# Transposes into an unread bank in TensorE's planned pauses, in the first part of the program

## The chip, the cores and the metric

The kernel runs on one core of a Trainium2 chip. The metric is the device time of one execution in microseconds, as the median of several runs. Five engines work side by side, each through a list of its own in order: TensorE (PE, with its weight loads shown as PEld), VectorE (DVE), ScalarE (ACT), GpSimd (POOL) and SyncE (SP), which here only issues DMAs.

## The reference

Attention with a causal mask and a decay bias, for 8 batches of 8 heads, 576 positions and a head width of 64, and behind it a feed-forward layer with an ELU between two products.

```python
cum = np.cumsum(np.maximum(s, 0.0), axis=-1)
bias = -(cum[:, :, :, None] - cum[:, :, None, :])
scores = np.where(causal, -1e9, q @ k.T / 8 + np.minimum(bias, 0.0))
attn = softmax(scores)                 # 576 x 576 for each head
x = (attn @ v)                         # heads side by side: 4608 x 512
h = x @ w_in                           # 512 x 2048
g = np.where(h > 0, h, np.exp(np.minimum(h, 0)) - 1)
out = g @ w_out                        # 2048 x 512
```

## The kernel before

The program has two kinds of work. Attention goes unit by unit. A unit is one batch and one pair of heads, or one head of it. The first three batches have their first 320 rows done as twelve "low" units in plain f32 (`prepare_low`, `scoring_low`, `weighing_low`), four to a batch; the remaining rows and batches follow as other units. The feed-forward layer goes in 12 chunks of 384 tokens (`moe_chunk`), each over 16 blocks of 128 hidden columns (`hidden`, line 1165, and `project`, line 1203). Products of the chunks stand between those of the later attention units and fill TensorE there. The first low units have no chunk work beside them yet, since no chunk's input is ready.

A low unit goes through these steps:

- SP loads keys (`kl`), queries (`ql`) and values (`vs`), and the row of decay sums for the keys (`kl<-aux` for the second unit, `kl<-aux_dram` after it). POOL fills the constant rows (lines 412 and 605). For the first unit DVE works out the sums itself (`kl_first`, lines 430 to 434).
- TensorE makes five score tiles `sc` of widths 128, 192, 192, 320 and 320 (line 869). DVE adds the mask and takes the minimum (line 872), ACT takes the exponential and the row sum (line 877), DVE inverts the sums (lines 882 and 883), and POOL, DVE or ACT scale the weights (lines 890, 892 and 894).
- TensorE turns the weights (`trl`, lines 680 and 694: transposes by `ident`), ACT or DVE copy them to `tl` (lines 381 and 382), and TensorE multiplies them by the values (`avl`, line 675). The weighing of a unit stands between the scores of the next one.

Beside this, the weights `w_in` and `w_out` are loaded in 32 pieces and split into two parts each, with several instructions on DVE, ACT and POOL for a piece (lines 363 to 374 and 531 to 537).

The order of all of it is planned when the program is built. `op` records an operation with the engines that could do it and their costs in nanoseconds; `Plan.issue` keeps a clock for each engine, takes the operation that could start earliest (a lower `prio` first among equals) and writes it behind the last one of its engine. Operations are held in order by that list, and a wait on a semaphore is added for each dependency on another engine. A buffer of one tag becomes free when the last user of its holder has been planned. Score tiles may borrow the banks of PSUM of the feed-forward part while those are idle:

```python
def score_bank(name):
    return plan.buf(ps, [P, 512], F32, name, tag="a", bufs=N_A,
                    others=[("h", N_H), ("o0", 1), ("o1", 1), ("o2", 1)])
```

So there are seven banks for scores and turned weights in the first part, two each of `a` and `h` and one each of `o0`, `o1` and `o2`, and an eighth for `avl`.

The constant `ident` is written by POOL at the start of the program, before anything of the plan.

Of the kernel before, what the change touches and what calls it, by code (L numbers as in the profile page):

```python
# [9 lines left out]
F32 = mybir.dt.float32  # L10
# [7 lines left out]
P = 128  # L18
# [26 lines left out]

N_FREE = 0


class Buf:

# [17 lines left out]


class Op:  # L70
    __slots__ = ("ways", "after", "before", "behind", "bufs", "new", "prio", "ready", "left")


class Plan:
# [33 lines left out]
    def op(self, prio, ways, reads=(), writes=(), late=()):  # L108

        o = Op()  # L110
        o.ways, o.prio = ways, (prio, len(self.ops))
        o.after, o.before, o.behind, o.bufs, o.new = set(late), [], [], set(), []
        firsts = set()
        for accesses, write in ((reads, False), (writes, True)):
            for a in accesses:
                b, part = a if isinstance(a, tuple) else (a, None)
                if not b.parts and b not in o.bufs:

                    n = self.tags.get(b.key, 0)
                    self.tags[b.key] = n + 1  # L120
                    o.new.append((b, n))
                    b.first = o
                firsts.add(b.first)
                if b not in o.bufs:
                    o.bufs.add(b)
                    b.users += 1
                for key, (writers, readers) in b.parts.items():
                    if part is None or key is None or key == part:
                        o.after.update(writers)
                        if write:  # L130
                            o.after.update(readers)
                writers, readers = b.parts.setdefault(part, ([], []))
                if write:
                    if part is None:
                        b.parts = {None: ([o], [])}
                    else:
                        b.parts[part] = ([o], [])
                else:
                    readers.append(o)
        o.after.discard(o)  # L140
        firsts -= o.after | {o}
        for d in o.after:
            d.before.append(o)
        for d in firsts:
            d.behind.append(o)
        o.left, o.ready = len(o.after) + len(firsts), {}
        self.ops.append(o)
        return o
# [8 lines left out]
    def issue(self):  # L157
        engines = sorted({self.ENGINE.get(w[0], w[0]) for o in self.ops for w in o.ways})
        port = 0.0
        free = dict.fromkeys(engines, 0.0)  # L160
# [12 lines left out]
        pending = [o for o in self.ops if not o.left]  # L173
        block = self.nc.cur_bb.bb
        last = {}
        n_done = 0
        while pending:
            best = None
            held = slots.get(self.signal, ())
            busy = free["PE"] > DYN_T or held and held[-1].users and not held[-1].others  # L180
            for o in pending:
                t = 0.0
                for b, k in o.new:
                    at = None
                    if taken[b.home] == k:
                        b.key, b.bufs = b.home, b.home_bufs
                        at = slot_free(b.key, b.bufs)
                    if b.others and not busy:
                        for key, bufs, *most in b.others:
                            if most and taken[key] > most[0]:  # L190
                                continue
                            other = slot_free(key, bufs)
                            if other is not None and (at is None or other < at):
                                at, b.key, b.bufs = other, key, bufs
                    if at is None:
                        break
                    t = max(t, at)
                else:
                    _, n, start = min(
                        (at + w[1] * self.BIAS.get(w[0], 1.0), i, at)  # L200
                        for i, w, at in (
                            (i, w, max(t, free[self.ENGINE.get(w[0], w[0])],
                                       self.ready(o, self.ENGINE.get(w[0], w[0])),
                                       port - self.PORT_LEAD if w[0] in self.PORT else 0.0))
                            for i, w in enumerate(o.ways)
                        )
                    )
                    rank = (start, o.prio)
                    if best is None or rank < best[0]:
                        best = (rank, o, n)  # L210
            assert best is not None, "no operation can be issued"
            (start, _), o, n = best
            engine, cost, trace = o.ways[n][:3]
            lag = 0.0
            end = start + cost
            if engine in self.PORT:
                port = end
            engine = self.ENGINE.get(engine, engine)
            if len(o.ways[n]) > 3:

                pipe = max(pipe, end) + o.ways[n][4] / RATE
                lag = pipe + o.ways[n][3] - end
            self.log.append((engine, start, end, o.prio))
            free[engine] = end
            for b, k in o.new:
                gone = skipped.setdefault(b.home, set())
                gone.add(k)
                while taken[b.home] in gone:
                    gone.remove(taken[b.home])
                    taken[b.home] += 1  # L230
                slots.setdefault(b.key, []).append(b)
            for b in o.bufs:
                b.until = max(b.until, end + lag)
                b.users -= 1
            pending.remove(o)
            for d in o.before:
                d.ready[engine] = max(d.ready.get(engine, 0.0), end + lag)
            for d in o.behind:
                d.ready[None] = max(d.ready.get(None, 0.0), start)
            for d in (*o.before, *o.behind):  # L240
                d.left -= 1
                if not d.left:
                    pending.append(d)
            at = len(block.instructions)
            trace()
            for i in block.instructions[at:]:
                if i.engine in last:
                    self.tc.add_manual_dep(
                        i, last[i.engine],
                        mybir.DependencyInfo(  # L250
                            mybir.DependencyClass.NoSync, mybir.DependencyReason.DATA
                        ),
                        reason="planned order",
                    )
                last[i.engine] = i.name
# [47 lines left out]
def kernel(  # L303
# [28 lines left out]
    DM, DF = w_in.shape  # L332
# [13 lines left out]
    plan = Plan(tc)  # L346
    op = plan.op
# [796 lines left out]
    def moe_chunk(ch, rows, xc, after):  # L1144
# [101 lines left out]
                t += n  # L1246
        return following

    decay_sums()
    zeros()  # L1250
    mask_tiles()
# [94 lines left out]
```

## Time and profile before

| what | value |
|---|---|
| median of 3 runs | 1131.26 us (1130.28, 1131.26, 1135.73) |
| profiled execution | 1133.43 us, of it the span 1131.7 us |
| mean granted TensorE clock of the profiled execution | 0.993 |
| TensorE matmuls: busy, instructions | 1096.9 us, 5992 |
| DVE, ACT, POOL busy | 843.3, 628.1, 451.1 us |
| DMA queue 1: moved, share of 16 engines | 155.27 MB, 59.6% |

The profile is of one execution. Its times count from the start of the span. A row of the timeline shows the start, the time from the first start to the last end of a run of like instructions (with their count behind an x), the engine, the line, and what was written from what; in brackets the idle time before it and what ended it. The runs of a row overlap their neighbours, since matmuls are pipelined. A row of the windows shows how long each engine was busy in a stretch, and the clock that TensorE was granted there as a share of the full one.

### The profile page before, as it was taken

The page shows a single profiled execution, that of the slowest core. Times are in us where ns is not written, and L with a number is a line of the kernel's source. Part 1 is how long each engine was busy: PE and PEld are TensorE (multiplying, and loading weights), DVE is VectorE, ACT ScalarE, POOL GpSimd, SP SyncE. Part 2 cuts the span into 40 slices and gives each one's busy share as a digit, 9 for nine tenths or more (in the row PEclk, how much of TensorE's full clock was granted, in tenths as well). Part 3 has the DMA queues.
Part 4 walks back from the last instruction along what each step waited for, and adds up shares of the span by engine and source line. Part 5 has one row for each costly group of instructions (what it writes and reads, how often), then busy time and mean ns, then how long its engine had stood idle before and what let it go on. Part 6 is the DMA issues. An engine that isn't in the chain of part 4 may idle for free.

```text
span 1131.7 us, 19748 instructions
## 1 busy us (share of the span) xinstructions
PE 1096.9 (97%) x5992; PEld 951.6 (84%) x5992; DVE 843.3 (75%) x2133; ACT 628.1 (55%) x1525; POOL 451.1 (40%) x657
## 2 busy tenths in 40 slices
PE   6888999999999999999999999999999999999998
PEld 5677877888788888788888888888888888999997
DVE  6888999778887877687977787878888888432322
ACT  4786766456555655555555555655655556433433
POOL 6664475336444433344434434525544433100000
PEclk8899999999999999999999999999999999999999
DMA  6887688756756855765555666567787686210000
GB/s 173 225 213 201 172 189 193 157 113 152 161 125 128 186 130 121 180 127 133 149 133 118 175 140 136 122 143 172 160 200 155 138 189 151 56 56 1 28 1 28
DMA packets 341689, 156.52 MB, mean 138 GB/s; under 512 B 266424, under 2 KB 320464, under 8 KB 341584
## 3 DMA queue, kind: packets, MB, share of 16 engines
q1 hardware_dynamic: 341584, 155.27, 59.6%
q8 instruction: 48, 0.79, 0.3%
q14 instruction: 57, 0.47, 0.1%
HBM read 79.66 MB, written 19.32 MB: 87 GB/s over the span
## 4 chain that ended last, share of the span: by engine, by line
PE 63%; DVE 6%; DMA 2%; issue 1%; ACT 1%; POOL 1%; SPq 0%; POOLq 0%; DVEq 0%; ACTq 0%
PE o L1203 26%; PE h L1165 25%; PE av L1000 7%; PE sc L869 5%; DVE p L930 2%; DMA stq<-in_qT_dram 1%; DMA T<-p 1%; DVE p L872 1%; DVE h L1187 1%; DVE xl L374 1%; DVE qs L374 0%; DVE x_None L1084 0%; DVE gl L1190 0%; DVE vs L374 0%; DVE g L1182 0%
## 5 line engine op out<-in xcount | busy, mean ns | idle before, releaser
L1165 PE MATMUL h<-xh,wi 128*128 128x384 f32 x1536 | 445.5, 340 | 1.4 <-DVE gl L1190 1.3
L1203 PE MATMUL o<-wo,gh 128*128 128x512 f32 x1152 | 362.5, 396 | 0.1
L1165 PEld LDWEIGHTS h<-xh,wi 128*128 128x128 f32 x1536 | 283.0, 188 | 9.9 <-DVE gl L1190 3.0
L1165 PE MATMUL h<-xl,wi 128*128 128x384 f32 x768 | 258.8, 337 | 0.0
L1203 PEld LDWEIGHTS o<-wo,gh 128*128 128x128 f32 x1152 | 207.3, 188 | 27.4 <-DVE mn L872 0.5
L1203 PE MATMUL o<-wo,gl 128*128 128x512 f32 x576 | 227.8, 395 | 1.0 <-DVE gl L1190 0.8
L1187 DVE SCALAR_TENSOR_TENSOR h<-h,g 128x384 f32<-128x384 f32 x192 | 107.9, 562 | 122.2 <-ACT g L1178 120.6
L1173 ACT ACTIVATE g<-h 128x384 f32<-128x384 f32 x192 | 94.1, 490 | 177.5 <-PE h L1165 167.4
L877 ACT ACTIVATE p<-p,mn 128x192 f32<-128x192 f32 (+1 forms) x232 | 144.9, 625 | 75.1 <-DVE mn L872 72.0
L930 DVE SCALAR_TENSOR_TENSOR p<-p,sm,p 128x512 f16<-128x512 f32 (+3 forms) x239 | 170.7, 742 | 7.6 <-POOL p L922 4.5
L1165 PEld LDWEIGHTS h<-xl,wi 128*128 128x128 f32 x768 | 144.6, 188 | 6.7
L922 POOL TENSOR_SCALAR p<-p,sm 128x512 f16<-128x512 f32 (+3 forms) x125 | 86.9, 702 | 134.3 <-DVE sm L883 53.1
L381 ACT CAST gh<-h 128x384 fp32r<-128x384 f32 x175 | 83.5, 477 | 87.8 <-DVE h L1187 86.6
L1190 DVE TENSOR_TENSOR gl<-h,gh 128x384 fp32r<-128x384 f32 x192 | 106.0, 552 | 32.9 <-ACT gh L381 31.7
L1203 PEld LDWEIGHTS o<-wo,gl 128*128 128x128 f32 x576 | 108.2, 188 | 25.8 <-DVE gl L1190 2.3
L872 DVE CUSTOM_DVE_ANT_0 p<-sc,maskw 128x192 f32<-128x192 f32 (+1 forms) x232 | 109.8, 483 | 25.8 <-PE sc L869 21.4
L1000 PE MATMUL av<-T,vs 128*128 128x256 f16 (+5 forms) x896 | 119.2, 285 | 2.9 <-DMA T<-p 2.1
L1000 PEld LDWEIGHTS <-vs 128*128 128x128 bf16 x896 | 79.7, 98 | 49.8 <-issue 14.3
L375 POOL TENSOR_TENSOR vs<-vs 128x320 f32<-128x320 f32 x72 | 61.0, 848 | 124.6 <-DMA vs<-in_vb_dram 72.1
L869 PE MATMUL sc<-kh,qs 128*128 128x192 f32 (+2 forms) x272 | 87.5, 326 | 2.9 <-DVE mn L872 2.5
L869 PE MATMUL sc<-k,q 128*128 128x192 f32 (+2 forms) x272 | 83.9, 312 | 2.2 <-DMA q<-qs 1.3
L1178 ACT ACTIVATE g<-g 128x384 f32<-128x384 f32 x138 | 72.5, 525 | 4.2
(145 smaller groups left out, 1365.3 us busy)
## 6 DMA issues: line engine op xcount, KB each, us to landing
stk<-in_kT_dram SPq DMA_DIRECT2D x64, 288.0 KB
vs<-in_vb_dram SPq DMA_DIRECT2D x64, 160.0 KB
stq<-in_qT_dram SPq DMA_DIRECT2D x40, 256.0 KB
w_i<-in_w_in_dram SPq DMA_DIRECT2D x16, 512.0 KB
w_o<-in_w_out_dram SPq DMA_DIRECT2D x16, 512.0 KB
out_dram<-ost SPq DMA_DIRECT2D x32, 256.0 KB
x_dram<-x_None SPq DMA_DIRECT2D x20, 288.0 KB
q<-qs SPq DMA_DIRECT2D x40, 128.0 KB
```

Of the source, the lines that this page charges most:

```text
L381: ("ACT", act_c(n), lambda: act.copy(dst(), src())),
L869: pe_.matmul(view(sc.v[:, :cw]), l, r, start=n == 0, stop=n == len(pairs) - 1)
L872: op(prio, [("DVE", 84 + dve_p(cw), lambda i=i, sc=sc: dve.tensor_tensor_reduce(pt.v[:, i * cw : (i + 1) * cw], sc.v[:, :cw], mv(i * cw, c ...
L877: op(prio, [("ACT", 480 + w / 1.2, lambda: act.activation(pt.v[:, :w], pt.v[:, :w], AF.Exp, bias=mn.v[:, n - 1 : n], scale=-1.0, accum_out ...
L922: ("Pool", 160 + 1.04 * n, lambda part=part: pool.tensor_scalar(part(t16, 0), own(part), sm.v[:, r], 1.0, ALU.mult, ALU.mult)),
L930: ("DVE-SB", dve_2(n), lambda part=part: dve.scalar_tensor_tensor(part(t16, 1), own(part), sm.v[:, r], part(t16, 0), ALU.mult, ALU.subtract)),
L1000: op(prio, [("PE", cost, lambda m=m, operands=operands, rows=rows: pe_.matmul(av.v[:rows, dst], *operands(), start=first and m == 0, stop= ...
L1165: pe_.matmul(hp.v[:, :TC], w_in_f[f].v[:, part, c * P : (c + 1) * P], xx.v[:, c, :TC], start=(c == 0 and m == 0), stop=(c == NCB - 1 and m ...
L1173: op(side, [("ACT", act_c(TC), lambda: act.activation(g.v[:, :TC], hp.v[:, :TC], AF.Exp))], [hp], [g])
L1187: op(side, [("DVE", dve_p(TC), lambda: dve.scalar_tensor_tensor(hp.v[:, :TC], hp.v[:, :TC], 0.0, g.v[:, :TC], ALU.max, join[0]))], [g], [hp])
L1190: op(side, [("DVE", dve_p(TC), lambda: dve.tensor_tensor(gl.v[:, :TC], hp.v[:, :TC], gh.v[:, :TC].bitcast(F32), ALU.subtract))], [hp, gh], ...
L1203: pe_.matmul(acc[i].v, g.v[:, tb], w_out_f[f].v[:, part], start=(f == 0 and m == 0), stop=(f == NF - 1 and m == 2),)
```

## The change

A function `fillers` gives the plan one transpose of `ident` into a tile `scratch` in PSUM, and 300 more of the same that read and write nothing else. They have the lowest urgency, a cost of 160 ns each in the plan, and are ranked 350 ns behind the time at which they could start: one is taken only where no other operation could start within 350 ns of it. Once TensorE's planned clock is past 60 us, those that are left are dropped. Nobody reads `scratch`. Its tag is `o2`, and it has that bank until the leftovers are dropped.

```diff
+FILL_T, GAP = 60e3, 350.0
+
+N_FILL = 300
+
...
-        o.ways, o.prio = ways, (prio, len(self.ops))
+        o.ways, o.prio, o.filler = ways, (prio, len(self.ops)), False
...
         while pending:
+            if free["PE"] > FILL_T:
+                for o in [o for o in pending if o.filler]:
+                    pending.remove(o)
+                    for b in o.bufs:
+                        b.users -= 1
+                if not pending:
+                    break
             best = None
...
-                    rank = (start, o.prio)
+                    rank = (start + GAP if o.filler else start, o.prio)
                     if best is None or rank < best[0]:
                         best = (rank, o, n)
             assert best is not None, "no operation can be issued"
             (start, _), o, n = best
+            if o.filler:
+                start -= GAP
...
+    def fillers():
+
+        scratch = plan.buf(ps, [P, DM], F32, "scratch", tag="o2")
+        op(-20, [("PE", 111.0, lambda: pe_.transpose(scratch.v[:, :P], ident, ident))], [], [scratch])
+        for n in range(N_FILL):
+            o = op(1e6 + n, [("PE", 160.0, lambda: pe_.transpose(scratch.v[:, :P], ident, ident))], [(scratch, None)], [])
+            o.filler = True
+
+    fillers()
     decay_sums()
```

In the built program 77 transposes stand, all on TensorE: 32, 23, 4, 5, 4 and 9 of them at six places. The other rows of TensorE and all rows of DVE, ACT, POOL and SP stand in the order of before. The lines of the changed kernel below are 13 higher than those of before for the same work (882 for 869, 707 for 694, 688 for 675).

TensorE's order at the start of the program, before, with the semaphores that a row waits for in brackets (`sc_0_...` are scores of the first unit, `sc_1_...` of the second, `trl_0` turned weights of the first; the last number of a name only counts tiles):

```order
L869 MATMUL sc_0_0_0_121<-kl_first,ql_0_85 128x128 [waits DMAHW2_49,DMAHW3_49,DVE_49,Pool_49]
L869 MATMUL sc_0_1_0_128<-kl_first,ql_0_85 128x192
L869 MATMUL sc_0_2_0_133<-kl_first,ql_0_85 128x192
L869 MATMUL sc_0_3_0_144<-kl_first,ql_0_85 128x320
L869 MATMUL sc_0_4_0_150<-kl_first,ql_0_85 128x320
L869 MATMUL sc_1_0_0_181<-kl_1_89,ql_1_99 128x128 [waits DMAHW5_49,DMAHW6_49,DMAHW2_49,Pool_49]
L869 MATMUL sc_1_1_0_188<-kl_1_89,ql_1_99 128x192
L869 MATMUL sc_1_2_0_194<-kl_1_89,ql_1_99 128x192 [waits DVE_49]
```

The same place of TensorE's order in the changed kernel:

```order
L1265 MATMUL scratch<-ident 128x128 [waits Pool_49]
L1267 MATMUL scratch<-ident 128x128 x31
L882 MATMUL sc_0_0_0_154<-kl_first,ql_0_93 128x128 [waits DMAHW2_49,DMAHW3_49,DVE_49,Pool_49]
L882 MATMUL sc_0_1_0_161<-kl_first,ql_0_93 128x192
L882 MATMUL sc_0_2_0_166<-kl_first,ql_0_93 128x192
L882 MATMUL sc_0_3_0_177<-kl_first,ql_0_93 128x320
L882 MATMUL sc_0_4_0_183<-kl_first,ql_0_93 128x320
L1267 MATMUL scratch<-ident 128x128 x23
L882 MATMUL sc_1_0_0_237<-kl_1_102,ql_1_115 128x128 [waits DMAHW5_49,DMAHW6_49,DMAHW2_49,Pool_49]
L882 MATMUL sc_1_1_0_244<-kl_1_102,ql_1_115 128x192 [waits DVE_49]
L882 MATMUL sc_1_2_0_250<-kl_1_102,ql_1_115 128x192 [waits DVE_49]
```

32 transposes stand ahead of the first score and wait for POOL alone, 23 stand behind the first unit's scores, and the second score of the second unit now waits for DVE, as its third did before.

TensorE's order at the end of the second unit's weighing, before (`trl_1_2` is the last piece of its turned weights, `avl_1` its products with the values, `sc_3` a score of the fourth unit):

```order
L675 MATMUL avl_1_314<-tl_1_303,vs_92 128x192
L694 MATMUL trl_1_2_354<-ident,p_112 128x128 [waits PE_49]
L694 MATMUL trl_1_2_354<-ident,pl_0_1_135 128x128
L675 MATMUL avl_1_314<-tl_1_303,vs_92 128x64 [waits DVE_49]
L675 MATMUL avl_1_314<-tl_1_303,vs_92 128x64
L869 MATMUL sc_3_0_0_375<-kl_3_246,ql_3_253 128x128 [waits DMAHW7_49,DMAHW6_49,DMAHW0_49]
```

The same place in the changed kernel:

```order
L688 MATMUL avl_1_370<-tl_1_359,vs_106 128x192
L707 MATMUL trl_1_2_410<-ident,p_141 128x128 [waits PE_49]
L707 MATMUL trl_1_2_410<-ident,pl_0_1_168 128x128
L1267 MATMUL scratch<-ident 128x128 x4
L688 MATMUL avl_1_370<-tl_1_359,vs_106 128x64 [waits DVE_49]
L688 MATMUL avl_1_370<-tl_1_359,vs_106 128x64
```

Four transposes stand ahead of the row that waits for DVE's copy of the turned weights.

TensorE's order at the last place, the weighing of the sixth unit, before:

```order
L694 MATMUL trl_1_1_700<-ident,pl_1_1_538 128x128
L694 MATMUL trl_1_1_700<-ident,pl_1_1_546 128x128
L694 MATMUL trl_1_2_717<-ident,p_112 128x128
L694 MATMUL trl_1_2_717<-ident,pl_1_1_546 128x128
L675 MATMUL avl_1_737<-tl_1_688,vs_92 128x128
```

The same place in the changed kernel:

```order
L707 MATMUL trl_1_1_765<-ident,pl_1_1_603 128x128
L707 MATMUL trl_1_1_765<-ident,pl_1_1_611 128x128
L1267 MATMUL scratch<-ident 128x128 x4
L707 MATMUL trl_1_2_786<-ident,p_141 128x128
L707 MATMUL trl_1_2_786<-ident,pl_1_1_611 128x128
L1267 MATMUL scratch<-ident 128x128 x9
L688 MATMUL avl_1_815<-tl_1_753,vs_106 128x128
```

Four transposes stand ahead of the last turned weights and nine behind them. The remaining five stand in the weighing of the fourth unit, between `trl_3` and `trl_3_0`.

More of the change, by code (lines that the diff above doesn't have):

```diff
@@ L70 @@
 class Op:
-    __slots__ = ("ways", "after", "before", "behind", "bufs", "new", "prio", "ready", "left")
+    __slots__ = ("ways", "after", "before", "behind", "bufs", "new", "prio", "ready", "left", "filler")
 class Plan:
```

## The prediction, made before the changed kernel ran

> **What bounds the kernel now.** I read the page first: span, busy engines, the TensorE clock by slice, the chain that ended last.
>
> ```profile
> span 1131.7 us, 19748 instructions
> PE 1096.9 (97%) x5992; PEld 951.6 (84%) x5992; DVE 843.3 (75%) x2133; ACT 628.1 (55%) x1525; POOL 451.1 (40%) x657
> ...
> PEclk8899999999999999999999999999999999999999
> ...
> PE 63%; DVE 6%; DMA 2%; issue 1%; ACT 1%; POOL 1%; SPq 0%; POOLq 0%; DVEq 0%; ACTq 0%
> ```
>
> TensorE bounds the whole, but the clock row is below 9 only in the first two slices (57 us). So I cut that part into windows, with edges moved until each held one clock. Columns: stretch, length, busy time (instructions) of PE, PEld, DVE, ACT, POOL, granted clock, DMA share, GB/s.
>
> ```profile
> 6.65:10.07 3.42, 3.42 (x10) 2.67 (x10) 2.89 (x8) 1.04 (x4) 3.23 (x10) 1.00 0.82 143
> 10.07:13.48 3.41, 0.35 (x2) 0.00 (x0) 3.31 (x13) 1.84 (x7) 1.80 (x4) 1.00 0.35 97
> 13.48:20.31 6.83, 6.12 (x21) 5.26 (x22) 1.78 (x10) 2.67 (x9) 1.12 (x3) 0.50 0.91 257
> 27.13:30.55 3.42, 1.83 (x13) 1.45 (x11) 3.39 (x10) 2.31 (x5) 2.24 (x5) 1.00 0.97 251
> 30.55:37.37 6.82, 6.13 (x22) 5.31 (x22) 3.55 (x13) 3.86 (x14) 3.68 (x6) 0.50 0.91 255
> 37.37:92.00 54.63, 48.95 (x287) 39.41 (x286) 49.19 (x163) 45.70 (x148) 34.55 (x74) 1.00 0.80 206
> ...
> 85.16:88.57 3.41, 2.19 (x15) 1.81 (x14) 3.34 (x8) 2.15 (x9) 2.73 (x8) 1.00 0.35 82
> ...
> 92.00:1131.70 1039.70, 1023.34 (x5606) 891.66 (x5604) 770.63 (x1900) 563.23 (x1321) 393.06 (x524) 1.00 0.59 133
> ```
>
> There are two spells at half clock, 13.48 to 20.31 and 30.55 to 37.37: both 6.83 us long, with starts 17.07 us apart, 2.5 times that length. So the clock is judged on a fixed raster of 3.41 us. The raster window ahead of each spell has little TensorE work: 0.35 us (10%) and 1.83 us (54%). A window with 2.19 us (64%) kept the clock. The limit lies between 54 and 64% busy, that is 1.2 to 1.6 us idle in 3.41 us. From 37 to 92 us the clock holds, and DVE is at 49.19 of 54.63 us (90%), as is PE. After 92 us PE is busy 98%: what the first part gains mostly stays gained.
>
> There is also a first cold burst that the clock column doesn't show.
>
> ```profile
> 6.47 3.95 PE L869 MATMUL sc<-kl_first,ql 128*128 128x128 f32 x10 [6.47 <-DVE kl_first L434]
> 8.31 2.11 PE L869 MATMUL sc<-kl_first,ql 128*128 128x320 f32 x4
> 14.19 2.04 PE L869 MATMUL sc<-kl,ql 128*128 128x128 f32 x6 [3.77 <-POOL p L890]
> ...
> 75.44 0.70 PE L869 MATMUL sc<-kl,ql 128*128 128x320 f32 x2
> ...
> 17.30 0.63 PE L694 MATMUL trl<-ident,p 128*128 128x128 f32 x2
> 17.73 0.63 PE L694 MATMUL trl<-ident,pl 128*128 128x128 f32 x2
> ...
> 61.85 0.38 PE L694 MATMUL trl<-ident,p 128*128 128x128 f32 x2
> 62.07 0.38 PE L694 MATMUL trl<-ident,pl 128*128 128x128 f32 x2
> ```
>
> Four instructions of width 320 take 2.11 us (0.53 each) at 8.31, two take 0.70 us at 75.44 (0.27 each, after about 0.16 of tail): the first five scores run at half pace though the column says 1.00. The transposes give a filler's price by their starts: two in 0.43 us cold (0.21 each), two in 0.22 us warm (0.11 each).
>
> **The change, part by part.** It adds 77 transposes at six places of PE's order and moves no other row on any engine. If TensorE's pace were all, warmth would be worth 1.9 us in the first burst (half of 3.95) and 3.1 us in each spell (half of 6.12 and 6.13), 8.1 us in all. What holds that up:
>
> ```profile
> 1.71 0.29 POOL masks.py:199 TENSOR_SCALAR_AFFINE_SELECT ident<-ident 128x128 f32<-128x128 f32 x1
> 7.40 0.29 DVE L872 CUSTOM_DVE_ANT_0 pl<-sc,masks 128x128 f32<-128x128 f32 x1 [0.53 <-PE sc L869]
> 9.75 0.88 POOL L469 MEMSET k<- 64x576 f32 x1
> 10.50 0.62 SPq L351 DMA_DIRECT2D kl<-in_kT_dram  x1
> 10.58 0.62 POOL L605 MEMSET ql<- 64x640 f32 x1
> 11.13 0.07 DVE L872 DVE_READ_ACCUMULATOR2_ANT mn<- 128x1 f32 x1
> 11.24 0.53 SPq L351 DMA_DIRECT2D ql<-in_qT_dram  x1
> 11.87 0.66 SPq L351 DMA_DIRECT2D kl<-aux  x1
> 12.80 0.15 DVE L882 TENSOR_SCALAR sml<-sml 128x5 f32<-128x5 f32 x1
> 13.92 0.53 POOL L890 TENSOR_SCALAR pl<-pl,sml 128x320 f32<-128x320 f32 x1
> ```
>
> *32 ahead of the first score.* They wait for ident alone, which POOL ends at 2.00. All cold they take 32 x 0.213 = 6.8 us, to 8.9; if a raster edge after 3.41 busy us warms them earliest (5.5 us), 16 cold and 16 warm end at 7.2. So they overrun the first score's start at 6.47 by 0.7 to 2.4 us; the burst, now warm, takes 1.9 to 2.0 and ends at 9.2 to 10.9 against 10.42. DVE's first reduction at 7.40 comes 0.4 to 2.1 us later, and its gapless chain up to the sums at 12.80 with it. This is covered: the last of these weights is ready at 14.45 (POOL at 13.92), and PE takes them at 17.30, 2.85 us later. If the spell goes, half of that cover goes too. Nor is there a gain: the second unit's first score at 14.19 needs the load at 11.87, which stands on SP behind a load that awaits POOL's fill of ql (10.58), and POOL is busy to 10.63 in any case. I take 0, between -0.5 and +0.8.
>
> *23 after the first burst.* Warm they take 23 x 0.107 = 2.5 us of a 3.77 us pause, so they cost nothing; 0.8 to 2.5 us of idle remain ahead of 14.19, depending on where the raster lies. Against the 1.2 to 1.6 us above, spell one is avoided in rather less than half of the positions.
>
> ```profile
> 27.82 0.27 PE L694 MATMUL trl<-ident,pl 128*128 128x128 f32 x1
> 29.68 0.66 PE L675 MATMUL avl<-tl,vs 128*128 128x64 f32 x4 [1.59 <-DVE tl L382]
> ...
> 31.31 0.48 PE L680 MATMUL trl<-ident,pl 128*128 128x128 f32 x1 [0.69 <-POOL pl L890]
> 58.91 2.40 PE L675 MATMUL avl<-tl,vs 128*128 128x128 f32 x14 [1.07 <-ACT xl L381]
> ```
>
> *4 ahead of the width-64 products.* They fill 0.43 of 1.59 us idle. In this raster the window 27.13:30.55 rises from 1.83 to 2.26 us (66%), just over what held; in the worst raster, 1.16 + 0.69 = 1.85 us stay idle and the spell comes. About even.
>
> *5, 4 and 9 around 42 and 57 us.* The clock is full there already. 18 x 0.107 = 1.9 us lie mostly in pauses such as the 1.07 us at 58.91; what doesn't fit delays PE, between nothing and the whole 1.9 us. I take 0.2, near to the row.
>
> *One accumulator bank less.* scratch holds a bank, so some scores wait for an older reduction of DVE. The second unit's wait for reductions of the first: the last of those ends at 11.20 (DVE at 11.13), at 13.3 with the delay above, and the scores start at 14.19. I take 0; if the cover went, the wait could cost one such reduction, about 0.5 us.
>
> *What an avoided spell is worth.* Its work, 6.12 us cold, needs 3.06 us warm and, at the 10% idle of the later windows, 3.4: 2.7 us saved. DVE sets the other bound: idle 5.05 us in spell one and 3.27 in spell two, against 0.7 in 6.83 at its later 90%, so 4.4 and 2.6 us can be recovered. The smaller of each gives 2.7 and 2.6; with the late sums and the pieces above, 2.5 us per spell, between 1 and 3.
>
> The profiled execution took 1133.43 us, 1.73 around its span, and the median is 1131.26, 2.2 lower: nearly one spell's worth. Since the raster need not stand alike in every execution, the median run may have one spell fewer; or the profile costs something. One spell avoided gives 1133.43 - 2.5 = 1130.9 by the first view and 1131.26 - 2.5 = 1128.8 by the second. I take the middle, 1129.8.
>
> [...] Do transposes count as work for the clock? The windows of lines 694 and 680 alone, then all of PE in the same stretch:
>
> ```profile
> 54.44:57.85 3.41, 1.70 (x10) 1.09 (x10) 1.00 1.04 265
> 54.44:57.85 3.41, 0.30 (x1) 0.14 (x1) 1.00 1.04 265
> 54.44:57.85 3.41, 2.87 (x16) 1.60 (x15) 3.29 (x12) 2.78 (x11) 3.22 (x6) 1.00 1.04 265
> ```
>
> Of 2.87 busy us, 2.00 are transposes; without them 0.87 us (26%) would be left, far below the 54% that lost the clock, and it stayed at 1.00. So they count here. [...]
>
> **The rivals.** *Both spells go:* 5.0 us, 1128.4 or 1126.3 by the two views, so 1127.3. For it: in the traced raster both windows end near 64 to 66%. Against: the raster moves, and a second unit started warm meets new waits for DVE and ACT.
> *Fillers stay cold and push work back (slower):* they would then last to 8.9, the first burst, cold, to 12.8, and 23 x 0.213 = 4.9 us to 17.7, past 14.19 by 3.5 us; the 18 late ones add up to 1.9. That gives 1131.26 + 3.5 to 5.4 = 1134.8 to 1136.7, say 1135.5. It decides from the point where fillers don't release the clock before the first burst ends. The window above speaks against it, though no trace shows a burst of transposes alone.
> *It doesn't do what it says:* fillers run warm, yet the idle left still loses both spells. Nothing gained, 0 to 1 us lost: 1132.
>
> **How the numbers follow.** One spell 0.43, both 0.26, none 0.22, cold fillers 0.09. Forecast 1129.8; the range 1126.3 to 1134.8 takes in the middle of every case but cold fillers. Half a per cent is 5.7 us, about what a measurement of this kernel can tell from no change. Faster than that (below 1125.6) needs both spells and the first burst: 0.08. Slower (above 1136.9) needs cold fillers and more: 0.04. Within: 0.88.
>
> **What would show it.** In the changed profile: the first fillers start near 2.1 us and their starts step from 0.21 to 0.11 us before 8.9; the first scores begin at 7.2 to 8.9, at 0.27 us per width 320; the second unit still starts near 14.2; the clock is 0.50 in one spell at most, and the 92 us mark moves about as much as the end. I am wrong if fillers keep 0.21 us throughout, if the second unit starts past 15 us, or if spells go and the end doesn't move.

## The result, and the profile after

| | median | runs | lowest to highest |
|---|---|---|---|
| before | 1130.67 us | 6 | 1128.23 to 1135.73 |
| changed | 1126.12 us | 6 | 1123.41 to 1127.68 |

The ratio is 0.9945, with an interval of 0.9926 to 0.9964: 4.6 us faster by the medians, where 1.5 us was forecast. The changed kernel run once more, unaltered, gave 1127.9 and 0.9962 [0.9946, 0.9979]. One of these nine executions took 1529.36 us at a granted clock of 0.655 and is left out here and below.

The page of the changed kernel, by the parts that were shown of before (span, busy engines, clock by slice, shares of the chain of waits):

```profile
span 1121.7 us, 19900 instructions
PE 1098.8 (98%) x6069; PEld 955.5 (85%) x6069; DVE 842.3 (75%) x2133; ACT 627.1 (56%) x1525; POOL 448.5 (40%) x657
...
PEclk9999999999999999999999999999999999999999
...
PE 73%; DVE 4%; DMA 3%; issue 1%; POOL 1%; ACT 1%; SPq 1%; POOLq 0%; DVEq 0%; ACTq 0%
```

The clock row has lost its two eights, and TensorE's share of the chain rose from 63 to 73%. The profiled execution took 1123.41 us, the lowest of its six, so the 10.0 us between the two profiled executions are more than the change is worth by the medians.

Windows of the changed kernel in steps of 3.41 us (columns as in the prediction), counted from 6.64, where its transposes change pace and the first record of its clock starts, then TensorE's timeline at the two planned pauses. Before's rows for the same places stand in the prediction.

```profile
10.06:13.47 3.41, 2.38 (x22) 2.14 (x20) 3.31 (x15) 2.37 (x9) 1.79 (x4) 1.00 0.39 110
13.47:20.30 6.83, 6.51 (x43) 5.94 (x44) 4.35 (x21) 5.33 (x18) 3.58 (x8) 1.00 0.96 271
23.71:27.12 3.41, 2.80 (x20) 2.46 (x18) 2.88 (x9) 2.75 (x8) 1.83 (x5) 1.00 0.19 60
27.12:30.53 3.41, 2.71 (x19) 2.21 (x19) 2.25 (x11) 2.87 (x10) 3.33 (x5) 1.00 0.95 234
30.53:37.36 6.83, 6.21 (x35) 4.68 (x33) 6.14 (x24) 4.66 (x16) 3.91 (x10) 1.00 1.11 315
```

```profile
2.05 0.48 PE L1265 MATMUL scratch<-ident 128*128 128x128 f32 x1 [2.05 <-POOL ident masks.py:199]
2.32 5.66 PE L1267 MATMUL scratch<-ident 128*128 128x128 f32 x31
7.82 2.12 PE L882 MATMUL sc<-kl_first,ql 128*128 128x128 f32 x10
9.77 2.67 PE L1267 MATMUL scratch<-ident 128*128 128x128 f32 x23
13.79 0.95 PE L882 MATMUL sc<-kl,ql 128*128 128x128 f32 x5 [1.34 <-issue]
...
25.19 0.60 PE L1267 MATMUL scratch<-ident 128*128 128x128 f32 x4
26.39 0.66 PE L688 MATMUL avl<-tl,vs 128*128 128x64 f32 x4 [0.61 <-DVE tl L395]
```

The window that first lost the clock before, with 0.35 us of work, now holds 2.38 us, and what follows it runs at full clock. The pause ahead of the width-64 products lay in 27.13:30.55 before. It now ends 3.3 us earlier, at 26.39 in place of 29.68, and so falls into another of these windows, 23.71:27.12, which holds 2.80 us; 27.12:30.53 holds other work. The first scores take 2.12 us (3.95 before) and the second unit starts at 13.79 (14.19).

Where the time went shows at a mark that both programs have in common, DVE's 201st instruction. Before, then the changed kernel:

```profile
79.92 0.08 DVE L872 DVE_READ_ACCUMULATOR2_ANT mn<- 128x1 f32 x1
```

```profile
74.80 0.08 DVE L885 DVE_READ_ACCUMULATOR2_ANT mn<- 128x1 f32 x1
```

Up to this mark 5.1 us are gained, which is what the rival "both spells go" had priced (5.0). From the mark to the end of the span it is 1131.7 - 79.92 = 1051.8 us before and 1121.7 - 74.80 = 1046.9 after: another 4.9 us, in a part where no instruction was changed and the clock was full in both. No term of the prediction held that.

### The profile page after: what moved, and what is told of

It reads as the page before. It is cut to its first block, busy times and chain, and to the rows that moved or that the text cites. A ratio compares the mean times of both kernels' runs of the same rounds, so it can differ in the third digit from the quotient of the medians.

```text
span 1121.7 us, 19900 instructions
## 1 busy us (share of the span) xinstructions
PE 1098.8 (98%) x6069; PEld 955.5 (85%) x6069; DVE 842.3 (75%) x2133; ACT 627.1 (56%) x1525; POOL 448.5 (40%) x657
## 3 DMA queue, kind: packets, MB, share of 16 engines
HBM read 79.66 MB, written 19.32 MB: 88 GB/s over the span
## 4 chain that ended last, share of the span: by engine, by line
PE 73%; DVE 4%; DMA 3%; issue 1%; POOL 1%; ACT 1%; SPq 1%; POOLq 0%; DVEq 0%; ACTq 0%
PE o L1216 29%; PE h L1178 29%; PE av L1013 8%; PE sc L882 6%; DVE p L943 1%; DMA T<-p 1%; DMA stq<-in_qT_dram 1%; DVE p L885 1%; DMA q<-qs 0%; DMA vs<-in_vb_dram 0%; DVE h L1200 0%; DVE xl L387 0%; DMA out_dram<-ost 0%; DMA x_dram<-x 0%; DVE qs L387 0%
```

## The experiments

All kernels keep the order of every other row on every engine; only the added instructions of TensorE differ. All but the two unaltered ones come from the changed kernel with one filter in `Plan.issue`, and a list of stretches of planned time in which fillers are let through:

```diff
+WHERE = [...]
...
             for o in pending:
+                if o.filler and not any(a <= free["PE"] < b for a, b in WHERE):
+                    continue
                 t = 0.0
```

G1 = (0, 6e3) holds the first 32 transposes, G2 = (7e3, 12e3) the 23 after the first burst, G3 = (24e3, 26e3) the 4, G4 and G5 = (35e3, 37e3) and (51e3, 56e3) the last 5 and 4 + 9. The one transpose that marks the bank always stays.

**The bank alone:** `WHERE = []`.

> scratch keeps its bank to the end of the plan's first 60 us as in the change, one transpose is written to it, and no filler is issued. If the gain is the clock's: two spells at 0.50, from about 13.5 and 30.5 us, each 6.8 us long, and a ratio to before of 1.000, within 0.003. If it comes from the other bank order or the shifted waits: no spells needed, ratio about 0.9945.

1130.73 us, ratio 1.000 [0.9981, 1.0019]. Holding the bank costs nothing that shows, within some 2 us.

**The first two groups:** `WHERE = [G1, G2]`, run twice.

> Only the 32 and the 23 are left. If each pause needs its own fillers: spell one is gone, spell two comes in the window that holds the pause ahead of the width-64 products, and about half of the gain is left, ratio 0.997 to 0.998. If spell two depends on where that pause lies in the raster: the program stands 3.3 us earlier there, the pause (about 25.2 to 26.4 us, 1.0 to 1.2 us idle) lies in another window (23.7 to 27.1) that stays over 60% busy, no spell at all, ratio 0.994 to 0.996.

> The 32 and the 23 once more, the kernel that had 0.9996 at a mean clock of 0.9985. If that was scatter: 0.996 to 0.998 this time. If the 23 behind the first burst do harm that takes the clock's gain back: 0.9985 to 1.001 again.

1131.08 us, 0.9996 [0.9979, 1.0013], and 1129.95 us, 0.9973 [0.9955, 0.9991]. The first is a miss: it gained nothing, though its trace held the full clock throughout. The second lies in the range of scatter.

**The second group alone:** `WHERE = [G2]`.

> Only the 23 behind the first burst are left. If the clock is judged window by window: the first burst is cold from 6.47 to about 10.4, the window 10.06 to 13.47 then holds the fillers (over 55% busy), no spell one, and with the shift no spell two; ratio 0.995 to 0.996, 0.4 us or less behind the change. If the first 32 are needed to bring the clock up: the fillers are cold, 23 x 0.213 = 4.9 us, the second unit starts past 15 us and the ratio is 1.000 or above.

1128.13 us, 0.9969 [0.9952, 0.9986]: a little less than foretold, with the full clock in the trace as foretold.

**The first group alone:** `WHERE = [G1]`, run twice.

> Only the 32 ahead of the first score are left. By the windows: the clock is lifted at about 6.6 us, the first burst is warm, the pause from about 9.8 to 13.8 us takes the clock at 13.5 all the same, both spells stay. Ratio 0.999 to 1.001. If the early lift were the source of the gain: ratio about 0.995.

> The 32 alone once more, the kernel that had 0.9971 at a mean clock of 0.997, no better than before. If the warm first burst is worth something of its own: 0.9965 to 0.998 again. If that was scatter: 0.999 to 1.001.

1126.46 us, 0.9971 [0.9952, 0.9991], and 1126.58 us, 0.9948 [0.9928, 0.9968]: the whole gain, though the window after the first burst is as empty as before and the clock was lost there in both traces. By the clock this is the wrong way round: 55 transposes, which keep the clock better, gain less than 32.

**Both kernels unaltered, once more:**

> The changed kernel once more, unaltered. If the clock is the whole cause: granted clock 1.000 in nearly every run, and a ratio of 0.997 to 0.998, since a run of before spends about 6 us at half clock on average and the runs so far put about 1.7 us on each 6.8 us of it. If the changed order itself brings something beside the clock: 0.9945 again, and runs of before at full clock stay about 3.5 us slower than this.

> The kernel before, unaltered, as if it were a new one: what is left of a difference where there is none. If runs scatter independently, the ratio is 1.000 within 0.0015. If a kernel keeps an offset of its own from one loading to the next, it may be off by 0.002 to 0.003 with an interval that leaves 1 out.

1127.9 us, 0.9962 [0.9946, 0.9979], and 1131.94 us, 1.0006 [0.9988, 1.0024]. The gain repeats, and an unaltered kernel shows none. In the trace of this second run of the changed kernel the clock was lost once, for 3.41 us at 71 us, and part of an early lead was given back at a store:

```profile
47.51 0.42 DVE L395 COPY xl<-avl 128x256 f32<-128x256 f32 x1 [2.19 <-DMA x_dram<-xl]
```

DVE waits 2.19 us for the one buffer `xl` to be stored; the first trace has no such wait.

**Does the work of the fillers count, or their number?** Four kernels: the 32 as products of width 2 instead of transposes; 32 transposes and the 23 as products of width 2; all groups but G2; and only the late groups.

```diff
-pe_.transpose(scratch.v[:, :P], ident, ident)
+pe_.matmul(scratch.v[:, :2], ident, ident[:, :2])
```

> The 32 products ahead of the first score are kept as instructions, at the same place, but each is a product of width 2 in place of a transpose of width 128, so they should take 1 to 2 us and leave the clock of the first burst as it was before. Earlier runs with 32 transposes there and none later gave 1126.8 us on average against 1131.3 for the kernel before, though the half-clock spells stayed, and no time was gained ahead of 80 us. Theory 'place of the instruction stream': what helps is that TensorE's later instructions stand 32 further back, so the fetches of instructions fall elsewhere against the loads; then this run gives 1126 to 1128 us. Theory 'warm first burst': what helps is the first scores at full pace and the schedule that follows; then nothing is gained here: 1130 to 1132 us.

> 32 transposes ahead of the first score as in the changed kernel; the 23 after the first burst become products of width 2 (a tenth of the work or less), 55 added instructions in all. With 23 transposes there the two earlier runs gave 1130.3 us on average, and without any there 1126.8. Theory 'place of the instruction stream': as with 55 transposes, 1129.5 to 1131 us. Theory 'the second group of transposes itself takes the gain back' (it sends the second unit ahead into a DMA wait): as with none, 1126 to 1128 us, with a half-clock spell near 13 us in the profile.

> The changed kernel without the 23 transposes after the first burst: 32 + 4 + 5 + 4 + 9, 54 added instructions. Theory 'place of the instruction stream': 54 is next to 55, so 1129.5 to 1131 us. Theory 'the second group takes the gain back': 1126 to 1127.5 us. By the clock alone the spell after the first burst stays in most executions, so 1 to 2 us above the changed kernel: 1127.5 to 1129.

> Only the late groups, 5 ahead of the width-64 products and 4 + 4 + 9 later (22 in all with the first that marks the accumulator bank); the first two pauses are left empty. By the clock alone the first spell stays and the second goes in about half of the executions: 1130 to 1131 us. Theory 'place of the instruction stream': 22 stands next to the 24 of the run with the second group alone, which gave 1128.0: 1127 to 1129 us. Theory 'warm first burst': no gain, 1130.5 to 1132.

They gave 1138.31 (1.006 [1.0039, 1.008]), 1129.37 (0.9988 [0.9971, 1.0005]), 1129.6 (0.999 [0.9974, 1.0005]) and 1129.39 us (0.9984 [0.9967, 1.0001]). The filters were `[G1]`, `[G1, G2]`, `[G1, G3, G4, G5]` and `[G3, G4, G5]`. The products of width 2 are no cheap stand-in: each is two products of TensorE, as the timeline of the first of these kernels shows.

```profile
2.50 13.37 PE L1271 MATMUL scratch<-ident 128*128 128x2 f32 x62
15.72 3.63 PE L886 MATMUL sc<-kl_first,ql 128*128 128x128 f32 x10
23.21 1.09 PE L886 MATMUL sc<-kl,ql 128*128 128x128 f32 x3 [3.86 <-POOL p L907]
```

62 take 13.37 us and push the first score from 6.47 to 15.72, so the two first runs miss their question. They do give a price: the second unit starts 8.8 us later than in before's two traces (14.38 in the mean) and the end comes 7.1 us later by the means of all runs, so some 0.8 us for each us, if nothing else of that change counts. The other two speak for the number: 54 added products without G2 stand where 55 stood, and 22 near 24.

**No-operations in place of products.** They hold a place in TensorE's program and do nothing.

```diff
+    def ahead():
+        for _ in range(N):
+            pe_.nop("shift")
+        return pe_.transpose(scratch.v[:, :P], ident, ident)
...
-        op(-20, [("PE", 111.0, lambda: pe_.transpose(scratch.v[:, :P], ident, ident))], [], [scratch])
+        op(-20, [("PE", 111.0, ahead)], [], [scratch])
```

N = 62, 106 and 152 with `WHERE = []`, and N = 44 with `WHERE = [G1]`:

> No filler; 62 no-operations and the one transpose that marks the bank stand ahead of the first score, 64 instructions as with 32 transposes (a product is a weight load and a matmul). Theory 'place of the instruction stream': the gain of the 32 transposes without their work, 1126 to 1128 us. Theory 'what the products do': as with the bank alone, 1130 to 1132 us.

> As the run with 62 no-operations, with 106: 108 instructions ahead, as with 54 products. Theory 'place of the instruction stream': 1129 to 1131 us, 2 us or more above the run with 62. Theory 'what the products do': 1130 to 1132 us, the same as with 62.

> As the run with 62 no-operations, with 152: 154 instructions ahead, as with the changed kernel's 77 products. Theory 'place of the instruction stream': 1126 to 1128 us (if the no-operations last beyond 6.47 us, later by four fifths of what the first score loses, by the run that pushed it back by 9.2 us and ended 7 us later). Theory 'what the products do': 1130 to 1132 us or later.

> The 32 transposes ahead of the first score, which alone gave 1126.8 us on average, with 44 no-operations ahead of them: 108 instructions, the place of 54 products. Theory 'place of the instruction stream': the gain is mostly gone, 1129 to 1131 us. Theory 'what the products do': it stays, 1126 to 1128 us, the no-operations lying in TensorE's wait for the identity matrix (up to 2.05 us).

They gave 1129.08 (0.9983 [0.997, 0.9996]), 1132.96 (1.0026 [1.001, 1.0042]), 1134.61 (1.0033 [1.0017, 1.005]) and 1133.17 us (1.003 [1.0013, 1.0048]). A no-operation lasts 0.07 us: the marking transpose starts at 5.36 behind 62, at 8.57 behind 106 and at 11.91 behind 152. In the last of these runs the second unit, at 20.30, is 6 us late.

```profile
11.91 0.45 PE L1272 MATMUL scratch<-ident 128*128 128x128 f32 x1 [11.91 <-issue]
12.16 4.18 PE L886 MATMUL sc<-kl_first,ql 128*128 128x128 f32 x10
20.30 2.05 PE L886 MATMUL sc<-kl,ql 128*128 128x128 f32 x6 [3.96 <-POOL pl L907]
...
83.64 0.08 DVE L889 DVE_READ_ACCUMULATOR2_ANT mn<- 128x1 f32 x1
```

By its span of 1130.2 us it needs 1046.6 us from the mark to the end, as the changed kernel does (1046.9), with no filler's work in it but the marking transpose. This traced execution was the lowest of its twelve, so the row bears witness and is no proof by itself. None of the four came out in the range that the mere number of added instructions had given. In three of them the no-operations weren't free: the first score starts 2.3 to 5.7 us later than before's 6.47. The run with 62 is the clean one, since its first score starts at 6.48. It gained 1.4 us by the means of its session (1129.15 against 1130.57), where 32 transposes, the same number of instructions, gained 4: something like a third of their gain comes without any of their work, and the rest doesn't.

The hardest figure is the last one: the 32 transposes, which gained 4 us, lose 2.5 us to the kernel before, by the means, once 44 no-operations stand ahead of them. The second unit starts 2.1 us later there (15.84 against 13.72), which leaves 4.5 of these 6.6 us even if each of those 2.1 us is paid in full.

**Where TensorE's instructions are fetched.** The page of both kernels has a DMA queue of its own for them:

```profile
q8 instruction: 48, 0.79, 0.3%
```

48 fetches move 0.79 MB, 16.4 KB each; for 5,992 products of a weight load and a matmul that is one fetch in some 125 products. They come at the same count of products from the start of the program: the last eight start behind 5,053 to 5,932 products before and behind 5,062 to 5,931 in the changed kernel, each pair within 9, so some 77 products earlier in the work that both share. Less data moves behind a fetch: in the twenty traces, over the 35 or 36 fetches of each between 100 and 900 us, queue 1 moved 72 to 106 GB/s in the 2 us after a fetch, against 160 to 203 in the us ahead of it and 150 to 152 in the mean of the whole stretch. What this can do shows at one product with `T` (weights turned by DMA). Windows, and behind them the waits of TensorE (total, times, longest), with 32 transposes and 44 no-operations, where a fetch starts at 285.40:

```profile
283.40:285.40 2.00, 2.00 (x11) 1.74 (x11) 1.50 (x6) 1.47 (x5) 0.00 (x0) 1.00 1.21 225
285.40:287.40 2.00, 1.85 (x12) 1.48 (x10) 1.85 (x7) 0.76 (x2) 0.00 (x0) 1.00 1.41 77
287.40:289.40 2.00, 0.67 (x4) 0.35 (x5) 0.79 (x3) 0.87 (x2) 0.00 (x0) 1.00 0.82 209
```

```profile
PE av L1017 <- DMA T<-p: 1.5, 1, 1.5
```

And windows and TensorE's timeline with the 32 transposes alone, where the same product starts at 284.90 and the fetch at 285.81:

```profile
283.00:285.00 2.00, 2.00 (x13) 1.74 (x13) 1.85 (x7) 0.77 (x3) 0.00 (x0) 1.00 0.92 214
285.80:287.80 2.00, 2.00 (x16) 1.70 (x15) 1.38 (x5) 1.13 (x4) 0.71 (x2) 1.00 0.18 41
```

```profile
284.90 2.10 PE L1017 MATMUL av<-T,vs 128*128 128x512 f16 x14
```

The last column falls from 225 to 77 GB/s after the fetch, `T` lands late, and TensorE waits 1.5 us. In the other kernel the fetch comes behind the need: the traffic falls to 41 GB/s, and nobody waits. The same product over all twenty traces: where the fetch stands 9 to 15 products ahead of it (11 traces), it starts 0.97 to 2.24 us after the product before it; where the fetch stands elsewhere (9 traces), 0.18 to 0.96 us; the means are 1.6 and 0.5. The two traces of the changed kernel are among the eleven (1.35 and 1.46 us), those of before among the nine (0.66 and 0.77). So this product shows how a fetch can delay TensorE, but here the change loses 0.7 us by it. Its gain must come from other products.

A count over all of them points the same way. TensorE's last 5,560 products are the same in every kernel, and the distance of each from the one before it can be compared with its median over the twenty traces. What exceeds the median adds up to 2.0 to 3.6 us in the three traces with 0 or 2 instructions added to TensorE, and to -1.5 to 0.0 us in the four with 154 or 156: 3.5 us less in the mean. Of these, 2.9 us fall on products that start 2 to 8 us after a fetch, which are a quarter of all; up to 2 us after one there is no difference. The bounds 2 and 8 were chosen with the figures in view.

**Foretelling single waits.** 26 no-operations ahead of the first transpose move each fetch by 13 products; in the changed kernel (`WHERE = [(0, 1e9)]`) and with `[G1]`.

> The changed kernel with 26 no-operations ahead of the first transpose, in idle time (26 x 0.073 = 1.9 us up to 2.05). Theory 'place of the fetches': each fetch comes 13 products earlier. The wait of the products with T near 285 us (av waits 1.0 us for the DMA of T in the changed kernel, with a fetch 14 products or 4.0 us ahead) goes, as in the four kernels whose fetch stood 54 products or more ahead or 6 after: 0.4 us or less. Other waits may come, so the time can be anything from 1125 to 1131 us. Theory 'what the products do': the same waits and 1126 to 1127.5 us.

> The 32 transposes ahead of the first score alone (1126.8 us on average) with 26 no-operations ahead of them, in idle time. Theory 'place of the fetches': the fetch near 76 us moves from 16 to about 29 products ahead of the transpose that waits 1.05 us near 80 us for the weights pl, and that wait shrinks to 0.4 us or less; the fetch near 286 us moves from 6 products behind the product with T to some 7 ahead of it, and that product's wait for the DMA of T comes up to between 0.5 and 1.5 us. Half way to the place of 44 no-operations, which gave 1133.2: 1128 to 1131 us. Theory 'what the products do': the same waits as without the no-operations and 1126 to 1127.5 us.

1129.05 us (0.9995 [0.9977, 1.0013]) and 1129.31 us (0.9983 [0.9969, 0.9998]), 2 to 3 us above the same kernels without them. They were meant to be free but delay the first transpose from 2.05 to 2.75. With the 32 alone, the wait for `pl` near 80 us:

```profile
PE trl L697 <- POOL pl L907: 1.0, 1, 1.0
```

becomes, in the waits with the 26 no-operations, the first of these rows, and a wait for `T` near 289 us comes up, the second:

```profile
PE trl L697 <- POOL pl L907: 0.3, 1, 0.3
...
PE av L1017 <- DMA T<-p: 1.1, 1, 1.1
```

Both as foretold. In the changed kernel the wait for `T` shrank from 1.0 to 0.6 us only, where 0.4 or less was expected: half a miss.

**All kernels side by side.** The place is the number of instructions added to TensorE (a transpose has two, a product of width 2 four). Over all 336 timed executions, a fit with one level for each kernel gives 0.61 (standard error 0.05) us of time for each us of full clock that the listed granted clock says was lost. "Levelled" takes this off, and 0.79 us (the price above, clock taken off) for each us that the second unit starts after 14.38; its standard error is 0.2 for before and 0.3 to 0.7 for the others. The row "32 of width 2" equals before by construction, since the price was taken from it, and "152 no-operations" rests on that price for 4.7 us.

| added to TensorE | place | runs, mean us | clock lost, us | second unit | levelled |
|---|---|---|---|---|---|
| nothing (before) | 0 | 153, 1130.9 | 3.6 | 14.38 | 1128.7 |
| the marking transpose | 2 | 10, 1131.3 | 4.2 | 14.62 | 1128.5 |
| late groups | 44 | 12, 1129.3 | 3.0 | 14.01 | 1127.8 |
| G2 | 48 | 10, 1127.9 | 1.9 | 14.26 | 1126.9 |
| G1 | 64 | 14, 1126.8 | 3.5 | 13.72 | 1125.2 |
| 62 no-operations | 64 | 12, 1129.2 | 2.5 | 14.53 | 1127.5 |
| G1, 26 no-operations | 90 | 12, 1128.9 | 4.0 | 14.82 | 1126.2 |
| all but G2 | 108 | 12, 1129.6 | 3.4 | 13.97 | 1127.9 |
| 106 no-operations | 108 | 12, 1133.2 | 3.5 | 16.53 | 1129.4 |
| G1, 44 no-operations | 108 | 12, 1133.4 | 3.5 | 15.84 | 1130.1 |
| G1, G2 | 110 | 17, 1130.3 | 1.8 | 14.13 | 1129.4 |
| 32 of width 2 | 128 | 10, 1137.9 | 3.7 | 23.21 | 1128.7 |
| all (changed) | 154 | 14, 1126.8 | 1.3 | 13.69 | 1126.6 |
| 152 no-operations | 154 | 12, 1135.1 | 4.3 | 20.30 | 1127.7 |
| G1, 23 of width 2 | 156 | 12, 1129.4 | 5.5 | 16.10 | 1124.7 |
| all, 26 no-operations | 180 | 12, 1129.8 | 1.8 | 15.14 | 1128.1 |

Kernels at about one place lie within 0.2 to 3.0 us of each other, whatever stands there; from place to place the mean goes from 1128.6 (0 and 2) to 1126.3 (64 and 90), to 1129.2 (108 and 110), to 1126.3 (154 and 156), and to 1128.1 (180). No version beat the changed kernel; the 32 transposes alone are level with it.

The listed clock leaves something out. It is counted from the first record of a trace, and TensorE is cold ahead of that: in the second trace of before the first record comes at 19.32, and two scores of width 320 still take 1.27 us at 16.61, though the page gives full clock there (0.70 at 19.58). So the executions of before lose more clock than is listed, and some of what is left to the place below belongs to the clock.

The place shows more plainly in the part of the traces that is the same in all kernels, from the mark (DVE's 201st instruction) to the end of the span. No price is taken off here; a star marks a trace that lost the clock in this part for 3.41 us, the last 4 us of the span not counted.

| place | mark to end, us, one figure for each trace |
|---|---|
| 0 and 2 | 1051.8, 1052.0*, 1051.1 |
| 44 and 48 | 1049.0, 1048.4 |
| 64 and 90 | 1048.6, 1046.4, 1049.6, 1049.1 |
| 108 to 128 | 1052.1*, 1049.4, 1051.6, 1049.0, 1051.1, 1049.4 |
| 154 and 156 | 1046.9, 1047.5, 1046.6, 1046.3 |
| 180 | 1052.8* |

The four traces at 154 and 156 are the changed kernel twice, the 152 no-operations, and the 32 transposes with 23 products of width 2. They lie within 1.2 us, and 3.6 us or more below the three at 0 and 2, whatever was added and however late the mark came (74.80 to 83.64). At 64 and at 108 to 128 the traces differ by up to 3.2 us, so the place isn't all.

## Why the prediction was wrong

**The clock: right in kind, a little dear.** One spell fewer was forecast, and by the listed clock before loses 3.6 us of full clock in a run, one spell of 6.83 us at half, and the changed kernel 1.3. At 0.61 us for each us a spell is worth 2.1, where 2.5 stood in the sum; what went is 2.3 us of listed clock, so 1.4 us. In the profiled pair both spells went, and the 5.1 us up to the mark are the rival's 5.0. That is partly luck: the second trace of the changed kernel has neither of these spells, only one at 71 us, and reaches the mark at 79.88.

The prediction took both spells from one trace. The first is regular: it went in all six traces with the 23 transposes, and in the fourteen without them the clock was lost there (twelve) or not yet up (two). "Rather less than half of the positions" was too low. The limit of 54 to 64% busy holds in the windows it was read from, but not in all: in the changed kernel 1115.97:1119.38 holds 1.60 us (47%), and the clock stayed at 1.00 to the end of the span, at 1121.7. The second stands in the first trace of before and in only one of the others, at 25.17 in the second run with the first two groups.

**Fillers lift the clock: right.** The clock rose ahead of any other matmul. Windows of the transposes alone in the changed kernel (length, busy time and count of those that touch the stretch, clock, DMA share, GB/s):

```profile
4.48:6.64 2.16, 2.16 (x12) 1.00 1.09 231
6.64:7.82 1.18, 1.18 (x12) 1.00 1.11 214
```

Up to 6.64 twelve take 2.16 us, from there twelve take 1.18 us, though the clock column says 1.00 for both. So the rival with cold fillers falls.

**The step that failed: "32 ahead of the first score ... Nor is there a gain ... I take 0, between -0.5 and +0.8".** Ahead of the second unit it held: that starts at 13.79, near the 14.19 foretold to stay. But these 32 by themselves gave 4 us with the spell still there, and the working had no place for that, since it costed an added instruction by the time it lasts and took "moves no other row on any engine" to mean that nothing else changes. What the runs showed in its place: 154 more instructions move every fetch of TensorE's program against the loads, and the part from the mark to the end, which holds nothing that was changed, comes out 4.7 us shorter (1051.9 to 1047.2 in the mean of two traces each). The four traces with that many instructions added, or two more, agree in this, one of them with no-operations and the marking transpose alone. That the place matters is shown by them, and by the 32 transposes, 4.9 us dearer after levelling with 44 no-operations ahead. That the data traffic falls behind a fetch is shown in twenty traces, and that the difference in TensorE's lost time lies mostly behind fetches, by the count over its products.

How much of the gain the place makes stays open. Of the 4.1 us between the means, the listed clock makes 1.4, the earlier start of the second unit some 0.5, and 2.1 are left, less than the 4.7 of the traces. The 62 no-operations got 1.2 us after levelling at a place where the transposes got 3.5, kernels at one place differ by up to 3 us, and only one wait was followed to its fetch in every trace. What else the 32 transposes bring isn't known.

**The other terms.** The bank at 0: right (1.000, within 2 us). The 23 "cost nothing": right in TensorE's time, and their window, with 2.38 us (70%), kept the clock. The 4: 0.61 us of idle stayed ahead of the products, and their window, 23.71:27.12 at 2.80 us (82%), kept it too. It wasn't the one foreseen (27.13:30.55 at 66%), since the program stands earlier there. Without the four, whose work is 0.43 us, it would hold some 2.4 us (70%), and of three traces that have the 23 but not the four, two kept the clock there as well. The delay of DVE's first reductions was covered, as said. "After 92 us ... what the first part gains mostly stays gained": 0.8 of a delay of the second unit reached the end, so yes; but more was gained there than carried over.

**The middle of two views, 1129.8.** With before's median of 1130.67 and 1.4 + 0.5 us, the clock and the start alone lead to 1128.8, inside the range; the rest took the time to 1126.12, just under its lower end of 1126.3. By how little is chance: the second run of the same kernel gave 1127.9, and the mean of its fourteen executions is 1126.8, both inside. The forecast gain of 1.5 us was too small by more than that, for want of the term above.

## What to carry to other kernels

Count an added instruction twice: for the time it takes, and for moving all later instruction fetches of its engine. This program, of fixed order and with TensorE busy 97% of its time, shifted by some 2 to 5 us of 1130 with the place of its instructions, so compare a small change with the same number of idle instructions, in free time, before its reasons are believed. And look at single waits with the fetch queue beside them, rather than at sums.

## What the runs showed of the hardware

- After a fetch of TensorE's instructions the data queue moved 72 to 106 GB/s for 2 us, in place of 150 (means of twenty traces).
- Products of width 2 didn't lift the clock. 62 of them kept TensorE busy for 13.37 us by the profile, yet the first scores behind them took 3.63 us, as cold as before (3.95); the same products took 0.13 us each behind warm work (46 in 5.91 us) and 0.21 us here.
- The spells at half clock lasted 3.41 or 6.83 us and began at other times in each trace: at 12.86, 13.47 and 14.40 us in three whose first scores start alike, at 6.47 or 6.48.
- The clock column of a page reads 1.00 ahead of the first record, though TensorE is cold there: 3.95 us for before's first scores, 2.12 us for the same work once warm.
- A no-operation on TensorE lasts 0.07 us (44 more of them, 106 for 62, put the marking transpose 3.21 us later), dearer than hoped: 26 in a pause of 2 us came out 0.7 us late.
